# Gated linear attention in chunks of 64 tokens on 64x64 tensor-engine tiles, with slot outputs as the weights of the combining product

## The chip, the cores and the metric

The kernel runs on one core of a Trainium2 chip. The metric is the device time of one execution in microseconds. The kernel before was timed in three runs: median 246.3 us, from 245.9 to 248.71. All tensors are float32.

## The reference

Two stages. The first is a gated linear attention over 4 batches x 8 heads x 768 tokens, head width 48; the second a soft mixture of experts on its output (3072 tokens of 384 values, 32 slots, 8 experts of 4 slots, hidden width 1024).

```python
f = 1 / (1 + exp(-f_logit))
for t in range(768):
    state = f[:, :, t, :, None] * state + outer(k[:, :, t], v[:, :, t])    # 48 x 48 per head
    y[:, :, t] = q[:, :, t] @ state
x = y as (3072, 384)
logits = x @ phi                                    # (3072, 32)
d = softmax of logits over the tokens;  slot_input = d.T @ x
slot_out[e] = relu(slot_input[e] @ w1[e]) @ w2[e]   # 8 experts, 4 slots each
c = softmax of logits over the slots;   out = c @ slot_out
```

## The kernel before

**Chunks.** The recurrence is computed in blocks of 128 tokens of one batch, all 8 heads together: 4 batches x 6 blocks = 24 blocks, n = 0 to 23. With g the running sum of -log f inside a chunk (its rows are called gate sums here), the products of a chunk use k * exp(g) and q * exp(-g), so that the decay between two tokens comes out of one product. Heads go in four pairs `a`; of a pair, head `r` = 0 lies on partitions 0 to 63 and `r` = 1 on 64 to 127, 48 of the 64 rows used.

**One block** (function `block`, L382), by the names under which the steps are planned:

- `exp`, `ln` (L373, L376): log(1 + exp(-f_logit)) on ACT (ScalarE), for two blocks at once after the first two.
- `cum` (L396) and `cumT` (L401): the gate sums twice on PE (TensorE), by a triangle of ones: once with tokens on the partitions (one product of 384 columns), once with the head's rows on the partitions (four products).
- `g`, `p` (L404, L407): their exponentials on ACT, 384 and 512 wide.
- `mk` (L413), `mq` (L416), `ends` (L410): k times one, q times the other, and the chunk's last gate, on POOL (GpSimd).
- `tk` (L421), `pk` (L424): k is turned, four transposes on PE, and copied out of PSUM.
- `kv` (L443): k-v products of the chunk, weights of 128 tokens x 64 columns. `sa`, `sm` (L446, L450): the new state on DVE (VectorE), an addition and a multiplication by the last gate.
- `sc` (L431): scores, 128 x 128 per head, 64 rows x 128 columns of weights. `mask` (L436): two DVE multiplications by the triangle, 4 heads x 128 columns each.
- `ia` (L459): intra, masked scores (weights of 128 x 128) times v (48 columns). `ie` (L468): inter, q (weights of 64 rows x 128 columns) times the state before the block (48 columns), added in the same bank. `py` (L471), put_y, copies y out.
- `tx`, `px` (L505, L508) turn the block's tokens for the mixture.

**Units.** After each fourth block a unit of 512 tokens goes through the mixture's first part (`unit`, L513): logits (`lg`, L524), exponentials, two turns (L536), the slot sums (`pi`, L543), the softmax over the slots and its turn into `cts` (L599). The softmax over the tokens needs one maximum for all units: units 1 to 4 are joined to a running maximum, sum and slot sum as they come (`j_min` to `j_new`, L549 to L565), six small DVE and two ACT instructions each; unit 5 is kept apart and both are added in the tail (`psi`, L667).

**Tail** (`tail`, L634): common maximum, `psi`, the experts' first products (`up`, L706), relu, turns (L721), the second products in three column parts (`down`, L740), the sum over a slot's rows (L752), then `combine` (L769): for each of three parts and six units four products with `cts` as weights (128 x 128) and 128 columns of slot outputs streamed. `put_f` (L775) copies to SBUF and `store` (L783) writes.

**Memory.** PSUM has eight banks: two pairs (names `pr`: scores and y), three single ones (`sg`, for everything else) and one for `kv`. Twelve buffers of 1 MB (`hm`) take w1 during the loop; the seven arenas of the loop (`aq` to `ak`) take the first seven pieces of w2 as the loop sets them free, and the `hm` buffers the rest.

**What sets the order.** The instructions are not issued in loop order. Each step is entered in `Plan` (L75) with the engines that may do it, a cost on each, what it reads and writes and a priority; `schedule` (L116) takes the step that can start first, the priority deciding between near ties, picks the engine where two may do it, and the bank. The result is a fixed list per engine; each engine runs its list in order and waits by semaphores. All loads are issued by SP in one such list.

## Time and profile before

| | |
|---|---|
| median of three runs | 246.3 us (245.9 to 248.71) |
| profiled execution | 245.48 us, span 243.8 us, mean granted clock 0.945 |
| instructions | 6448, of them 2708 matmul records on PE |
| DMA | 50.89 MB, mean 209 GB/s |
| loads per block | q 256 KB, k 192 KB, v 192 KB, f 384 KB for two blocks |

The page of the profile lists busy time by engine; PEld is PE's weight loads, which overlap its products. A row of the order in time gives start and length in us, engine, line, operation, tiles (what it writes <- what it reads), for PE its array tile as rows*columns, the shape streamed, how many were merged, and in brackets how long the engine stood idle before and for whom. A group row ends in its total busy time, the mean ns of one, and the idle time before. An f32 product appears as two matmul records, a transpose as one. Records of products that run side by side in the array overlap, so the time of a group is read from its start to the next one's start, or from the span of many less the length of one.

### The profile page before, as it was taken

What the parts mean: (1) busy time and instruction counts of PE and PEld (TensorE: products, weight loads), DVE (VectorE), ACT (ScalarE), POOL (GpSimd) and SP (SyncE); (2) the same over time, 40 slices, a digit from 0 to 9 for tenths busy, and PEclk for the clock granted to TensorE, in tenths of its full rate; (3) what the DMA queues carried; (4) which work ended last, traced back from release to release, by engine and by line L of the source; (5) the groups of instructions that cost most, each with busy time, mean ns of one, the idle gap of its engine ahead of it and who ended that gap; (6) DMA issues with size and microseconds to landing.
All of it is one profiled execution on the core that took longest, in us unless ns stands there. A gap on an engine that the chain in (4) does not pass through costs nothing.

```text
span 243.8 us, 6448 instructions
## 1 busy us (share of the span) xinstructions
PE 230.1 (94%) x2708; PEld 190.1 (78%) x2708; DVE 103.2 (42%) x244; ACT 89.7 (37%) x193; POOL 57.7 (24%) x88
## 2 busy tenths in 40 slices
PE   8999999999999999999999999999988799999870
PEld 8789889878888789879897898888977333498760
DVE  3354543346443564357425485345370322224230
ACT  3454353436532255343524545433322211103330
POOL 2134432306320263213323431521400000000000
PEclk9999999999998999999999999999997569999965
DMA  6999366268753873366836663720785939905562
GB/s 177 350 347 332 120 189 226 84 218 249 259 170 108 265 246 125 105 179 270 242 116 197 239 221 125 235 79 3 272 321 203 376 95 378 421 12 205 238 264 88
DMA packets 17862, 50.89 MB, mean 209 GB/s; under 512 B 2336, under 2 KB 8736, under 8 KB 14752
## 3 DMA queue, kind: packets, MB, share of 16 engines
q1 hardware_dynamic: 17824, 50.39, 60.2%
q8 instruction: 23, 0.38, 0.6%
q14 instruction: 15, 0.12, 0.1%
HBM read 45.66 MB, written 4.72 MB: 207 GB/s over the span
## 4 chain that ended last, share of the span: by engine, by line
PE 93%; ACT 2%; DVE 1%; issue 1%; DVEq 0%
PE pr L459 17%; PE pr L431 10%; PE sg L401 10%; PE pr L468 9%; PE sg L396 8%; PE sg L706 5%; PE sg L443 5%; PE sg L740 5%; PE sg L421 5%; PE sg L769 4%; PE sg L505 4%; PE sg L306 3%; PE sg L524 2%; PE sg L543 2%; PE sg L599 1%; PE sg L721 1%
## 5 line engine op out<-in xcount | busy, mean ns | idle before, releaser
L459 PEld LDWEIGHTS pr<-av,as 128*128 128x128 f32 x384 | 45.0, 192 | 2.1 <-issue 1.0
L459 PE MATMUL pr<-av,as 128*128 128x48 f32 x384 | 45.8, 272 | 0.0
L436 DVE TENSOR_TENSOR as<-pr,tri 128x512 f32<-128x512 f32 x48 | 31.5, 686 | 28.2 <-PE pr L431 28.2
L401 PEld LDWEIGHTS sg<-tri,al 128*128 128x128 f32 x192 | 24.5, 196 | 3.6 <-issue 0.6
L401 PE MATMUL sg<-tri,al 128*128 128x128 f32 x192 | 27.2, 286 | 0.0
L468 PE MATMUL pr<-st,aq 64*128 64x48 f32 x320 | 22.5, 281 | 0.0
L396 PE MATMUL sg<-al,tri 128*128 128x384 f32 x48 | 21.2, 523 | 0.2 <-ACT al L376 0.2
L468 PEld LDWEIGHTS pr<-st,aq 64*128 64x128 f32 x320 | 19.9, 191 | 1.2 <-issue 0.2
L413 POOL TENSOR_TENSOR ap<-ak,gb 128x384 f32<-128x384 f32 x12 | 12.2, 1014 | 35.1 <-ACT gb L404 35.1
L471 ACT COPY xr<-pr 128x384 f32<-128x384 f32 x14 | 6.7, 479 | 32.7 <-PE pr L468 30.0
L471 DVE COPY xr<-pr 128x384 f32<-128x384 f32 x10 | 5.6, 558 | 25.4 <-PE pr L468 22.0
L413 POOL TENSOR_TENSOR ap<-ak 128x384 f32<-128x384 f32 x11 | 11.0, 1004 | 21.6 <-ACT ak L404 21.5
L421 PE MATMUL sg<-ident,ap 128*128 128x128 f32 x96 | 15.1, 280 | 0.3 <-DVE ap L413 0.3
L416 POOL TENSOR_TENSOR aq<-aq,af 128x512 f32<-128x512 f32 x11 | 14.0, 1272 | 0.0
L416 POOL TENSOR_TENSOR aq<-aq,ap 128x512 f32<-128x512 f32 x11 | 14.0, 1270 | 0.0
L443 PE MATMUL sg<-av,ap 128*64 128x48 f32 x320 | 13.9, 231 | 0.0
L431 PE MATMUL pr<-aq,ap 64*128 64x128 f32 x192 | 13.8, 284 | 0.0
L443 PEld LDWEIGHTS sg<-av,ap 128*64 128x64 f32 x320 | 11.3, 141 | 3.2 <-issue 2.3
L431 PE MATMUL pr<-aq,av 64*128 64x128 f32 x192 | 13.7, 282 | 0.0
L505 PE MATMUL sg<-ident,xr 128*128 128x128 f32 x72 | 12.8, 288 | 0.8 <-ACT xr L471 0.8
L431 PEld LDWEIGHTS pr<-aq,av 64*128 64x128 f32 x192 | 11.7, 188 | 2.1 <-issue 1.6
L508 ACT COPY xT<-sg 128x384 f32<-128x384 f32 x17 | 8.2, 480 | 12.9 <-PE sg L505 12.9
(144 smaller groups left out, 312.9 us busy)
## 6 DMA issues: line engine op xcount, KB each, us to landing
hm<-in_w_dram SPq DMA_DIRECT2D x17, 1024.0 KB, 7.9
aq<-in_q_dram SPq DMA_DIRECT2D x24, 256.0 KB, 3.1
ak<-in_k_dram SPq DMA_DIRECT2D x24, 192.0 KB, 4.1
av<-in_v_dram SPq DMA_DIRECT2D x24, 192.0 KB, 3.8
af<-in_f_dram SPq DMA_DIRECT2D x11, 384.0 KB, 4.5
out_dram<-hm SPq DMA_DIRECT2D x6, 512.0 KB, 3.0
out_dram<-hm SPq DMA_DIRECT2D x6, 256.0 KB, 3.1
af<-in_w_dram SPq DMA_DIRECT2D x1, 1024.0 KB, 4.8
```

Source lines behind the costliest of these rows:

```text
L396: nc.tensor.matmul(bank(("cum", n))[:, :384].rearrange("p (h d) -> p h d", h=H), tri, l[:, :, :D], start=True, stop=True)
L401: nc.tensor.matmul(pc[:, a], l[:, 2 * a : 2 * a + 2].rearrange("p r d -> p (r d)"), tri, start=True, stop=True)
L413: tt(e)(kp_[:, :, :D], k_, g_, op=ALU.mult)
L416: tt(e)(flat(q_), flat(q_), flat(p_), op=ALU.mult)
L421: nc.tensor.transpose(pk[:, a], kp_[:, 2 * a : 2 * a + 2].rearrange("p r d -> p (r d)"), ident)
L431: nc.tensor.matmul(ps[:, r, a], kt_[rs, a], q_[rs, a], start=True, stop=True)
L436: tt(e)(sc_[:, r], ps[:, r], tri.unsqueeze(1).broadcast_to([128, PR, 128]), op=ALU.mult)
L443: nc.tensor.matmul(pk[DP * r : DP * r + DP, a], kp_[:, 2 * a + r], v_[:, 2 * a + r], start=True, stop=True)
L459: nc.tensor.matmul(py[:, r, a], sc_[:, r, a], v_[:, 2 * a + r], start=a == 0, stop=first and a == PR - 1, skip_group_check=True,)
L468: nc.tensor.matmul(py[:, r, a], q_[rs, a], s_old[rs, a], start=False, stop=a == PR - 1, skip_group_check=True)
L471: copy(e)(x_.rearrange("p (a r e) -> p r a e", a=PR, r=2), y_at())
L505: nc.tensor.transpose(px[:, c], x_[:, 128 * c : 128 * c + 128], ident)
```

## The change

- **Chunk of 64.** `C` becomes 64; a block stays 128 tokens (`BT`) and holds two chunks. k comes from memory like q, with the head's rows on the partitions (padded from 48 to 64, so 256 KB per block).
- **64x64 tiles.** Gate sums, scores, k-v, inter and intra become 16 products per block each, on weights of 64 (or 48) rows x 64 (k-v: 48) columns. Chunk `c` and head `r` choose the quarter of the array: rows from one, columns from the other. [...]
- **Gate sums once.** `sums_l` replaces `cum` and `cumT`: only the form with the head's rows on the partitions, 64 columns per chunk; both exponentials read it, 512 wide each. `mk` multiplies k in place (512 wide); `tk` turns it for `kv`; the scores read k unturned.
- **State twice per block.** Two additions and two multiplications on DVE, one pair per chunk; `ends` takes two copies. One mask of 512 columns for two.
- **PSUM.** Three pairs (gate sums, k-v, y, scores share them) and two single banks; the pairs are zeroed at the start on DVE. `ie` now begins y's bank and `ia` ends it; scores are entered after `ie`.
- **No joins.** Each unit keeps its maximum, sum and slot sums; `psi` adds six units in the tail.
- **Combining.** `s4`, the slot outputs, becomes the weights (128 columns) and `cts` of four blocks is streamed, 512 columns: 18 products for 72. The output is stored transposed (384 x 3072).
- **Planner.** Costs of many steps change; six arenas instead of seven take pieces of w2.

```diff
-    plan = Plan({"pair": [0, 1], "one": [0, 1, 2], "kv": [3]})
+    plan = Plan({"pair": [0, 1, 2], "one": [0, 1]})
...
+    def c_kv(e):
+        for t in pairs:
+            nc.vector.memset(t, 0.0)
...
-        def cum(e):
-            nc.tensor.matmul(bank(("cum", n))[:, :384].rearrange("p (h d) -> p h d", h=H), tri, l[:, :, :D], start=True, stop=True)
-
-        def cumT(e):
-            pc = bank(("cumT", n)).rearrange("p (a t) -> p a t", a=PR)
-            for a in range(PR):
-                nc.tensor.matmul(pc[:, a], l[:, 2 * a : 2 * a + 2].rearrange("p r d -> p (r d)"), tri, start=True, stop=True)
+        def sums_l(e):
+            ps = bank(("cum", n))[:, :, : PR * C].rearrange("p c (a t) -> p c a t", a=PR)
+            for a in range(PR):
+                for c in range(2):
+                    for r in range(2):
+                        nc.tensor.matmul(ps[half[r], c, a], l_[half[c], 2 * a + r], tri[half[c]], start=True, stop=True)
...
         def scores(e):
...
-                    nc.tensor.matmul(ps[:, r, a], kt_[rs, a], q_[rs, a], start=True, stop=True)
+                        nc.tensor.matmul(ps[half[c], r, a], k_[rows[r], a, half[c]], q_[rows[r], a, half[c]], start=True, stop=True)
...
         def kv(e):
...
-                    nc.tensor.matmul(pk[DP * r : DP * r + DP, a], kp_[:, 2 * a + r], v_[:, 2 * a + r], start=True, stop=True)
+                for j in steps:
+                    for r in range(2):
+                        h, c = 2 * a + r, j ^ r
+                        nc.tensor.matmul(pk[C * r : C * r + D, j, a], kp_[half[c], h, :D], v_[half[c], h], start=True, stop=True)
...
         def inter(e):
...
-                    nc.tensor.matmul(py[:, r, a], q_[rs, a], s_old[rs, a], start=False, stop=a == PR - 1, skip_group_check=True)
+                for j in begun:
+                    for r in range(2):
+                        nc.tensor.matmul(py[half[j], r, a], q_[rows[r], a, half[j ^ r]], s_[j][rows[r], a], start=a == 0, stop=False, skip_group_check=True)
...
         def intra(e):
...
-                        py[:, r, a], sc_[:, r, a], v_[:, 2 * a + r], start=a == 0, stop=first and a == PR - 1, skip_group_check=True,
+                            py[half[j], r, a], sc_[half[c], r, a], v_[half[c], 2 * a + r], start=j not in begun and a == 0,
+                            stop=a == PR - 1, skip_group_check=True,
...
+        add(f"ie{n}", {"PE": 0.52}, inter, r=[*[S[j] for j in begun], Q, "kv0"], psum=("y", n), kind="pair", prio=T(n, 3.9))
+        add(f"sc{n}", {"PE": 0.52}, scores, r=[K, Q], psum=("sc", n), kind="pair", prio=T(n, 4), after=[len(plan.ops) - 1])
...
         def combine(p, x):
...
-                    nc.tensor.matmul(pf[:, g], cts[:, UB * x + g], s4[:, CUT[p] : CUT[p + 1]], start=True, stop=True)
+            return lambda e: nc.tensor.matmul(
+                bank(("cb", p, x))[:w], s4[:, CUT[p] : CUT[p + 1]], cts[:, UB * x : UB * x + UB].rearrange("p n t -> p (n t)"), start=True, stop=True,
+            )
```

How the order moves, at three places. A row gives line, operation, tiles with bank numbers, the shape written and how many stand together. First PE in the middle of the loop, before: turning k, k-v, gate sums, intra, inter, turning x and scores of neighbouring blocks alternate.

```order
L421 MATMUL sg_66<-ident,ap 128x128 x4
L443 MATMUL sg_67<-av,ap 64x48 x8
L396 MATMUL sg_64<-al,tri 128x384
L459 MATMUL pr_62<-av,as 128x48 x8
L468 MATMUL pr_62<-st_89,aq 128x48 x8
L401 MATMUL sg_65<-tri,al 128x128 x4
L396 MATMUL sg_66<-al,tri 128x384
L505 MATMUL sg_64<-ident,xr 128x128 x3
L431 MATMUL pr_63<-aq,av 128x128 x8
```

PE in the loop with the change (L403 gate sums, L429 turning k, L442 scores, L453 k-v, L472 inter, L482 intra, L521 turning x, L539 logits):

```order
L472 MATMUL pr_64<-st_90,aq 64x48 x2
L482 MATMUL pr_63<-av,ap 64x48 x16
L442 MATMUL pr_62<-aq,ak 64x64 x16
L521 MATMUL sg_65<-ident,xr 128x128 x3
L403 MATMUL pr_63<-tri,al 64x64 x16
L482 MATMUL pr_64<-av,ap 64x48 x16
L403 MATMUL pr_62<-tri,al 64x64 x16
L521 MATMUL sg_66<-ident,xr 128x128 x3
L403 MATMUL pr_64<-tri,al 64x64 x16
L429 MATMUL sg_65<-ident,ak 128x128 x4
L539 MATMUL sg_66<-xT,phs 32x128 x12
L453 MATMUL pr_63<-av,ap 48x48 x16
```

The groups on the pairs are all of 16 products now, some of them stand next to each other, and the gate sums of up to three blocks stand ahead of one block's k-v.

Second, DVE in the same part, before: masks two by two, and one state step (L446, L450) per block.

```order
L436 TENSOR_TENSOR as<-pr_63,tri 128x512 x2
L446 TENSOR_TENSOR sa<-sg_67,st_88 128x192
L450 TENSOR_TENSOR st_89<-sa,pend 128x192
L436 TENSOR_TENSOR as<-pr_62,tri 128x512 x2
L424 COPY av<-sg_65 128x512
L508 COPY xT<-sg_64 128x3x128
L446 TENSOR_TENSOR sa<-sg_67,st_89 128x192
```

DVE with the change (L445 mask, L456 and L461 the state's addition and multiplication, L524 the copy of turned x):

```order
L445 TENSOR_TENSOR ap<-pr_62,tri 128x512
L456 TENSOR_TENSOR sa_91<-pr_63,st_89 128x192
L461 TENSOR_TENSOR st_90<-sa_91,pend 128x192
L456 TENSOR_TENSOR sa_92<-pr_63,st_90 128x192
L461 TENSOR_TENSOR st_87<-sa_92,pend 128x192
L524 COPY xT<-sg_66 128x3x128
L445 TENSOR_TENSOR ap<-pr_64,tri 128x512
```

Between two blocks' masks stand four state instructions that read each other's results.

Third, PE in the tail, before: `down` (L740) of the next part and `combine` (L769) of the last, on three single banks.

```order
L740 MATMUL sg_66<-av,xr 32x128 x16
L769 MATMUL sg_64<-s_118,cts 128x128 x4
L769 MATMUL sg_65<-s_118,cts 128x128 x4
L740 MATMUL sg_66<-hm_75,xr 32x128 x16
L769 MATMUL sg_64<-s_118,cts 128x128 x4
```

PE in the tail with the change (L728 `down`, L753 `combine`):

```order
L728 MATMUL sg_65<-av,xr 32x128 x16
L753 MATMUL sg_66<-cts,s_118 128x512
L728 MATMUL sg_65<-hm_73,xr 32x128 x16
L753 MATMUL sg_66<-cts,s_118 128x512
L728 MATMUL sg_65<-hm_74,xr 32x128 x16
```

`down` holds one of the two single banks, and the combining products share the other.

## The prediction

> **What bounds the kernel now.** I read the page's busy shares and its chain of waits first, then the busy times by stage, then the order in time of TensorE in one stretch of the loop over blocks. The page:

> ```profile
> span 243.8 us, 6448 instructions
> ...
> PE 230.1 (94%) x2708; PEld 190.1 (78%) x2708; DVE 103.2 (42%) x244; ACT 89.7 (37%) x193; POOL 57.7 (24%) x88
> ...
> PE 93%; ACT 2%; DVE 1%; issue 1%; DVEq 0%
> ```

> TensorE (PE) is 93% of the chain that ended last; no other compute engine is busy for half the span. By stage (stretch and its length in us; busy time of PE, weight loads, DVE, ACT, POOL; then granted clock, DMA share, GB/s):

> ```profile
> 7.00:188.00 181.00, 178.52 (x2008) 154.30 (x2007) 85.72 (x197) 75.95 (x164) 55.47 (x69) 0.99 0.61 202
> 188.00:244.00 56.00, 45.67 (x668) 29.91 (x668) 15.44 (x41) 11.37 (x25) 0.40 (x1) 0.80 0.61 233
> 10.00:20.00 10.00, 9.79 (x107) 8.16 (x104) 5.62 (x11) 4.61 (x10) 2.99 (x4) 1.00 1.00 352
> ```

> The loop fills PE (178.5 of 181 us, clock 0.99) and leaves the others half idle. It begins with the first gate sum and ends with the last put_y:

> ```profile
> 7.16 0.81 PE L396 MATMUL sg<-al,tri 128*128 128x384 f32 x2
> ```

> ```profile
> 187.42 0.48 ACT L471 COPY xr<-pr 128x384 f32<-128x384 f32 x1 [2.83 <-PE pr L468]
> ```

> So the run is 7.2 us of start, 180.7 us of loop (7.16 to 187.90) and 55.9 us of mixture tail; the result lists 245.5 us for this execution, 1.7 more than its span and 0.8 under the median of 246.3. What a block costs PE is read from start to next start:

> ```profile
> 100.13 1.13 PE L431 MATMUL pr<-aq,av 64*128 64x128 f32 x16
> 101.19 0.66 PE L421 MATMUL sg<-ident,ap 128*128 128x128 f32 x4
> 101.68 0.49 PE L505 MATMUL sg<-ident,xr 128*128 128x128 f32 x3
> 102.10 0.67 PE L443 MATMUL sg<-av,ap 128*64 128x48 f32 x16
> 102.70 0.91 PE L396 MATMUL sg<-al,tri 128*128 128x384 f32 x2
> 103.45 1.88 PE L459 MATMUL pr<-av,as 128*128 128x48 f32 x16
> 105.26 0.86 PE L524 MATMUL sg<-xT,phs 128*32 128x128 f32 x24
> ```

> ```profile
> 122.67 1.09 PE L468 MATMUL pr<-st,aq 64*128 64x48 f32 x16
> 123.69 1.16 PE L401 MATMUL sg<-tri,al 128*128 128x128 f32 x8
> 124.69 0.60 PE L421 MATMUL sg<-ident,ap 128*128 128x128 f32 x4
> ```

> Scores 1.06, turning k 0.49, turning x 0.42, k-v products 0.60, gate sums 0.75 + 1.00, intra 1.81, inter 1.02. (An f32 product is two records, a turn one.) With k-v and inter in 20 of 24 blocks that is 6.9 us, 165 in all; the 15.6 left of the loop are the six units, 0.65 per block. The loop is the sum of PE's groups, with next to nothing waited for.

> **The change, part by part.** Intra is dear because its 128-column weights set the pace, not the 48 columns that it streams. What a 64-column tile costs is seen where two stand side by side in the array:

> ```profile
> L443 PE MATMUL sg<-av,ap 128*64 128x48 f32 x320 | 13.9, 231 | 0.0
> ...
> L667 PE MATMUL sg<-wd,pin 128*32 128x32 f32 x48 | 1.1, 245 | 0.3 <-ACT pin L546 0.3
> L740 PE MATMUL sg<-al,xr 128*32 128x128 f32 x32 | 1.1, 276 | 0.0
> ```

> 16 records of L443 span 0.67 and one lasts 0.231: (0.67 - 0.231)/15 = 29 ns per record, 58 for the two that run together. The change cuts rows too, so four 64x64 tiles can stand together: 58/4 = 14.6 ns per record. Each of the five groups (gate sums, scores, k-v, inter, intra) has 16 products, 32 records: 0.47 us, and with the 0.13 that L443 loses at its ends (0.60 - 0.47) 0.60. The trace has no 64x64 tile; that four run as two do is an assumption, which the rivals take up. Five groups 3.0, turns 0.49 + 0.42, units 0.65: 4.6 us, less 0.1 for the halves missing at each sequence's ends; 4.46 x 24 = 107 us. Lower, if neighbours of one tile shape lose less between them. These two groups start 0.90 apart, of which 32 records at (1.08 - 0.276)/31 = 26 ns are 0.83:

> ```profile
> 213.01 1.08 PE L740 MATMUL sg<-ak,xr 128*32 128x128 f32 x32
> 213.91 1.06 PE L740 MATMUL sg<-af,xr 128*32 128x128 f32 x32
> ```

> At 0.05 lost in place of 0.13, and k-v's 48-column weights at three quarters of 64, PE falls to 95. In the new order about half of the neighbours share a shape: I take 101 (95 to 107).

> The other engines inherit the loop. ACT, DVE and POOL rows that bear on it:

> ```profile
> L407 ACT ACTIVATE af<-sg 128x512 f32<-128x512 f32 x12 | 7.2, 597 | 11.1 <-PE sg L401 9.4 <-POOL ap L413 1.7
> ...
> L404 ACT ACTIVATE gb<-sg 128x384 f32<-128x384 f32 x12 | 5.9, 491 | 10.6 <-PE sg L396 9.9 <-POOL pend L410 0.6
> ```

> ```profile
> L436 DVE TENSOR_TENSOR as<-pr,tri 128x512 f32<-128x512 f32 x48 | 31.5, 686 | 28.2 <-PE pr L431 28.2
> L450 DVE TENSOR_TENSOR st<-sa,pend 128x192 f32<-128x192 f32 x16 | 7.1, 442 | 1.6
> L446 DVE TENSOR_TENSOR sa<-sg,st 128x192 f32<-128x192 f32 x16 | 5.7, 354 | 5.4 <-PE sg L443 5.3
> ```

> ```profile
> L416 POOL TENSOR_TENSOR aq<-aq,ap 128x512 f32<-128x512 f32 x11 | 14.0, 1270 | 0.0
> L413 POOL TENSOR_TENSOR ap<-ak,gb 128x384 f32<-128x384 f32 x12 | 12.2, 1014 | 35.1 <-ACT gb L404 35.1
> ...
> L410 POOL COPY pend<-af 128x4 f32<-128x4 f32 x12 | 2.8, 233 | 37.6 <-ACT af L407 37.6
> ```

> ACT: the gate exponentials go from 384 to 512 wide (24 x 0.106 = 2.5) and the order gives it five more put_y at 0.48, while the joins' eight small exponentials go: 76 becomes about 79. DVE: 24 masks fewer (-16.5), 24 state additions (+8.5) and 22 state multiplications (+9.7) more, the joins' 24 instructions gone (at L446's 0.354, -8): 86 becomes some 80. POOL: k is 512 wide (24 x 0.26 = 6) and the ends take two copies (5.6): 55 becomes 67. DMA: 24 blocks of q and k (256 KB each), v and f (192 KB each) and 12 MB of w1 are 34 MB, at the 352 GB/s of 10:20 some 97 us. So behind PE's 101 stand DMA with 97, DVE and ACT with 80: a loop that had one limit has two, with two more at 80%.

> PE will therefore not be busy throughout. Block 0 now takes from 7.2 to this row's end:

> ```profile
> 15.89 0.48 ACT L471 COPY xr<-pr 128x384 f32<-128x384 f32 x1 [0.83 <-PE pr L459]
> ```

> These are 9.2 us of handing on, in which the new PE has little more than one block's 4.2 us to do: 4 us idle in front, some 3 at the end. In between I put 4 to 5 us of waits: the order on each engine is fixed, POOL's 1.27 stands once ahead of the block's k and once ahead of its q, and every second block brings ACT a double exponential ahead of a gate sum. 101 + 11.5 = 112.5. What is late next is the side that PE waited on last: inter reads the state after two additions and two multiplications in a row on DVE (0.8 us per pair), with masks, and so intra, queued behind them.

> The start stays at 7.2: PE's warm products end there, and DVE's added memsets (three pairs of 1024 columns, at L436's rate about 4 us) end before. Without that cover they would cost what they overrun.

> In the tail psi adds all six units where two stood, 96 records more:

> ```profile
> 194.86 0.55 PE L667 MATMUL sg<-wd,pin 128*32 128x32 f32 x24
> ```

> ```profile
> 190.00:200.00 10.00, 8.44 (x97) 3.77 (x93) 4.16 (x19) 1.88 (x7) 0.40 (x1) 0.51 0.60 216
> ```

> (0.55 - 0.245)/23 = 13 ns each, at half the clock: +1.3 us. Combining has 18 products that stream 512 columns where 72 streamed 128. With 128-column weights one of the 72 costs about L459's 1.81/16 = 0.11, 8 us in all; one of the 18 costs no less than that (2 us) and no more than L396's 0.375 per record for 384 columns would give at 512, 0.5 (9 us). Their copies out of PSUM stay 18, on two single banks instead of three, so I take -0.5 (-4 to +1). w2's pieces and the stores keep their places behind the same steps.

> Sum: 7.2 + 112.5 + 55.9 + 1.3 - 0.5 + 1.7 = **178.1 us**.

> **Rivals.** *The fixed order binds* (0.22). Three PSUM pairs hold four things of each block: the gate sums (PE 0.6, two exponentials of 0.6), k-v (0.6, then 0.35, 0.44, 0.35 on DVE), y (inter 0.6, scores 0.6, mask 0.69, intra 0.6, put_y 0.48) and the scores (0.6, mask 0.69). With 0.15 for each handover, an assumption, that is 2.1 + 2.1 + 3.6 + 1.5 = 9.3 us, or 3.1 per block on three pairs, three quarters of PE's 4.2; loads at 97 of 101 leave even less. If these queue up and DMA gets three quarters of 352 GB/s, the loop is 130 us and the time 196. For it: every share rises. Against: none exceeds PE's.

> *PE alone binds* (0.15): 96 us and 7 at the ends, 168. So far PE's work hid every wait; but then the others had half their time.

> *The tiles run, but fewer at once* (0.07). L740's 26 ns per record may be a floor for a record and not its 128 columns: 160 records x 11.3 ns x 24 = +43, 221. Two at a time, 29 ns: +56, 234. Against: L667 starts records 13 ns apart, and that at half the clock. [...]

> *The tiles run one after the other* (0.03), and the change doesn't do what it says: if row tiles and column tiles can't be mixed, a record costs 58 ns, +44 x 160 x 24 = +169: 347, slower. This decides from 14.6 + 68,000/(160 x 24) = 32 ns per record on; L443's 29 for two tiles speaks against it.

> The forecast keeps 0.53.

> **How the numbers follow.** The forecast's own range is 170 to 188 (PE 95 to 107, idle time 9 to 17, tail -4 to +1). With the PE-bound and the queueing case, 166 to 199 leaves out just under 2 in 10. Faster by over 2% (about what a measurement of this kernel tells from no change) is all but the serial case and accidents of its size: 0.95; within 2% 0.02, slower 0.03.

> **What would show it.** Right: groups of 32 records on 64x64 tiles 0.5 to 0.6 us apart; PE busy near 100 us in a loop of 105 to 120; DVE and ACT near 70% busy in it, DMA share above 0.8; a tail of 56 to 58 us. Wrong: records 25 ns or more apart; gaps before PE's groups that together pass 20 us, ended by DVE's state steps, ACT's gate exponentials or loads; a granted clock in the loop well under 0.99, as the tail's 0.51 already is.

## The result, and the profile after

The changed kernel takes 235.0 us (median of four runs, 231.4 to 236.3) where the kernel before takes 246.3: a ratio of 0.944 (95% interval 0.929 to 0.960). It is faster, but by a sixth of what was forecast: 178 us, with a range of 166 to 199. The profiled execution is the longest of the four, 236.26 us. The ratios leave out executions more than 1.5% above the fastest of their kernel; of these four that leaves 231.4 and 234.8.

First the page of the changed kernel: span, busy times, granted clock in 40 slices, the queue that brings instructions, and the chain that ended last.

```profile
span 234.5 us, 10707 instructions
...
PE 179.6 (77%) x4814; PEld 133.6 (57%) x4814; DVE 101.0 (43%) x231; ACT 95.6 (41%) x203; POOL 69.7 (30%) x113
...
PEclk9955595699855999958678579999997589999985
...
q8 instruction: 40, 0.66, 1.1%
...
PE 63%; issue 15%; DVE 13%; ACT 5%; DVEq 0%; POOLq 0%
```

The same two rows of the page before:

```profile
PEclk9999999999998999999999999999997569999965
...
q8 instruction: 23, 0.38, 0.6%
```

Three things are new. PE is busy for 77% of the span instead of 94%. Its clock, 0.99 in the loop before, drops to half again and again (a 5 in the row PEclk, 0.80 over the loop). And 15% of the chain is "issue", time in which PE waits for nothing that the profile shows. PE's products and weight loads have gone from 2 x 2708 to 2 x 4814, and the queue that brings code moves 40 packets of 16 KB for 23.

By stage (columns: stretch and its length, busy time of PE, weight loads, DVE, ACT, POOL, granted clock, DMA share, GB/s), with the loop's last put_y as the border:

```profile
7.00:173.00 166.00, 130.21 (x4069) 104.18 (x4068) 85.56 (x188) 78.53 (x169) 67.53 (x95) 0.80 0.65 217
173.00:234.50 61.50, 43.52 (x710) 23.66 (x710) 11.11 (x33) 14.65 (x30) 0.40 (x1) 0.85 0.63 247
```

The loop takes 166 us (forecast 112.5): PE is busy 130.2 (forecast 101) and idle 35.8 (forecast 11.5). ACT and POOL have the work that was forecast (79 and 67), DVE some 6 us more than its 80. What PE waited for, all lines with "issue" in the loop (L655 and L728 belong to the tail), and the two largest other waits (engine, what it was to write, line, what ended the wait: us in total, times, longest):

```profile
PE pr L403 <- issue: 8.7, 5, 3.2
PE pr L482 <- issue: 5.2, 3, 2.5
PE pr L472 <- issue: 5.0, 3, 1.9
PE sg L655 <- issue: 4.0, 1, 4.0
PE pr L482 <- DVE ap L445: 3.8, 10, 0.8
PE sg L521 <- issue: 3.6, 1, 3.6
PE pr L472 <- DVE st L461: 2.8, 3, 1.5
PE sg L728 <- issue: 1.9, 1, 1.9
...
PE pr L442 <- issue: 1.0, 1, 1.0
PE sg L539 <- issue: 0.9, 1, 0.9
...
PE pr L453 <- issue: 0.8, 1, 0.8
```

The loop's issue waits are 8.7 + 5.2 + 5.0 + 3.6 + 1.0 + 0.9 + 0.8 = 25.2 us, in 15 stops. That leaves 10.6 us of idle time of every other kind, nearly the 11.5 of the forecast. The clock explains the rest. Six stretches of the loop are at half clock, and their lengths (17.07, 10.24, 13.66, 6.83, 6.83 and 10.24 us) are whole multiples of 3.41 us. The first two, and the sum of the six:

```profile
11.34:28.41 17.07, 13.89 (x321) 12.13 (x322) 8.10 (x16) 7.08 (x14) 7.70 (x9) 0.50 0.78 284
35.23:45.47 10.24, 7.77 (x179) 6.29 (x175) 4.26 (x8) 3.56 (x8) 7.83 (x11) 0.50 0.69 246
...
sum 64.87, PE 53.27 PEld 42.12 DVE 25.07 ACT 23.12 POOL 31.61; mean PE 8.88 PEld 7.02 DVE 4.18 ACT 3.85 POOL 5.27
```

PE is busy there for 53.3 us. If the same work takes half of that at full clock (an estimate; stage G below shows 213 ns per record at 0.50 for 112 before the fall), 26.6 us are lost, and 130.2 - 26.6 = 103.6 is an estimate of what the loop's work costs at full speed: the forecast's 101. So the 53.5 us by which the loop missed are 25 us of stops, 27 us of half clock, and 1 to 2 us of everything else.

What a stop looks like, in the order in time of PE:

```profile
65.97 1.10 PE L403 MATMUL pr<-tri,al 64*64 64x64 f32 x32
66.85 0.86 PE L453 MATMUL pr<-av,ap 64*48 64x48 f32 x32
67.64 0.47 PE L521 MATMUL sg<-ident,xr 128*128 128x128 f32 x1
71.73 0.69 PE L521 MATMUL sg<-ident,xr 128*128 128x128 f32 x2 [3.62 <-issue]
```

The three turns of L521 are one step: same input, same output tile, same semaphores. After the first, PE stops for 3.62 us and goes on. Nothing in the program stands between the two. Counted from the start, the stops lie at PE's instruction (products, weight loads and the semaphore instructions between them) 450, 706, 1218, 1474, 2497, 2754, 3010, 3777 and so on: distances of 256 or a multiple, give or take one. A packet of queue q8 has 16 KB (40 move 0.66 MB), and PE mostly resumes 1.2 to 1.5 us after one has landed; that one packet holds the 256 instructions, 64 bytes each, is an estimate from these distances and sizes. (The expectations below speak of 34 us of stops within groups: there the whole distance from record to record was counted, here only the idle time.)

### The profile page after: what moved, and what is told of

Read it like the earlier page. It is cut to its first block, busy times and chain, and to the rows that moved or that the text cites. A ratio compares the mean times of both kernels' runs of the same rounds, so it can differ in the third digit from the quotient of the medians.

```text
span 234.5 us, 10707 instructions
## 1 busy us (share of the span) xinstructions
PE 179.6 (77%) x4814; PEld 133.6 (57%) x4814; DVE 101.0 (43%) x231; ACT 95.6 (41%) x203; POOL 69.7 (30%) x113
## 4 chain that ended last, share of the span: by engine, by line
PE 63%; issue 15%; DVE 13%; ACT 5%; DVEq 0%; POOLq 0%
PE pr L403 8%; PE pr L482 7%; PE sg L429 6%; PE pr L442 6%; PE pr L472 5%; PE sg L694 5%; PE sg L728 5%; PE sg L521 5%; DVE ap L445 3%; PE pr L453 3%; PE sg L539 3%; PE sg L316 3%; PE sg L753 2%; DVE st L461 2%; ACT hm L759 2%
## 5 line engine op out<-in xcount | busy, mean ns | idle before, releaser
L421 POOL TENSOR_TENSOR ak<-ak,av 128x512 f32<-128x512 f32 x11 | 14.0, 1269 | 55.0 <-ACT av L407 28.0
L403 PE MATMUL pr<-tri,al 64*64 64x64 f32 x768 | 22.4, 259 | 8.9 <-issue 8.7
L424 POOL TENSOR_TENSOR aq<-aq,pt 128x512 f32<-128x512 f32 x22 | 28.7, 1303 | 0.4 <-ACT pt L407 0.4
L482 PE MATMUL pr<-av,ap 64*64 64x48 f32 x768 | 20.2, 247 | 9.1 <-issue 5.2
L472 PE MATMUL pr<-st,aq 48*64 48x48 f32 x704 | 20.3, 240 | 8.0 <-issue 5.0
L403 PEld LDWEIGHTS pr<-tri,al 64*64 64x64 f32 x768 | 18.4, 166 | 12.3 <-issue 11.5
L482 PEld LDWEIGHTS pr<-av,ap 64*64 64x64 f32 x768 | 16.8, 158 | 14.2 <-DVE ap L445 7.7
L445 DVE TENSOR_TENSOR ap<-pr,tri 128x512 f32<-128x512 f32 x24 | 16.6, 690 | 19.1 <-PE pr L442 18.7
L472 PEld LDWEIGHTS pr<-st,aq 48*64 48x64 f32 x704 | 17.1, 153 | 12.4 <-issue 7.3
L442 PE MATMUL pr<-aq,ak 48*64 48x64 f32 x768 | 20.2, 241 | 1.0 <-issue 1.0
L461 DVE TENSOR_TENSOR st<-sa,pend 128x192 f32<-128x192 f32 x38 | 19.7, 519 | 2.5
L429 PE MATMUL sg<-ident,ak 128*128 128x128 f32 x96 | 19.6, 344 | 1.4 <-DVE ak L421 1.4
L456 DVE TENSOR_TENSOR sa<-pr,st 128x192 f32<-128x192 f32 x40 | 14.2, 355 | 14.6 <-PE pr L453 7.1
L521 PE MATMUL sg<-ident,xr 128*128 128x128 f32 x72 | 15.5, 328 | 5.1 <-issue 3.6
L442 PEld LDWEIGHTS pr<-aq,ak 48*64 48x64 f32 x768 | 17.1, 152 | 3.3 <-issue 3.3
L421 POOL TENSOR_TENSOR ak<-ak,af 128x512 f32<-128x512 f32 x12 | 15.3, 1271 | 11.7 <-issue 8.4
L453 PE MATMUL pr<-av,ap 64*48 64x48 f32 x704 | 15.5, 224 | 0.8 <-issue 0.8
L429 PEld LDWEIGHTS sg<-ident,ak 128*128 128x128 f32 x96 | 13.1, 172 | 3.2 <-DVE ak L421 1.6
L521 PEld LDWEIGHTS sg<-ident,xr 128*128 128x128 f32 x72 | 8.9, 161 | 9.6 <-issue 3.9
L407 ACT ACTIVATE pt<-pr 128x512 f32<-128x512 f32 x24 | 14.3, 597 | 0.0
```

Of the source, the lines that this page charges most:

```text
L403: nc.tensor.matmul(ps[half[r], c, a], l_[half[c], 2 * a + r], tri[half[c]], start=True, stop=True)
L407: nc.scalar.activation(dst.rearrange("p a (c t) -> p c a t", c=2), src, AF.Exp, scale=sign)
L421: tt(e)(flat(k_), flat(k_), flat(g_), op=ALU.mult)
L424: tt(e)(flat(q_), flat(q_), flat(p_), op=ALU.mult)
L429: nc.tensor.transpose(pk[:, a], k_[:, a], ident)
L442: nc.tensor.matmul(ps[half[c], r, a], k_[rows[r], a, half[c]], q_[rows[r], a, half[c]], start=True, stop=True)
```

## Experiments

In these, a piece is 256 PE instructions. The theory to be tested: PE's code arrives piece by piece, and the dense tiles use it up faster than it comes; the stops in turn bring the clock down. The rivals: the tiles themselves lower the clock; transfers alone delay the code; or PE's work and ordinary waits set the time.

### Products alone, without the kernel

> This kernel computes nothing of the reference: it only runs stages of products on PE and stores zeros. Stages, with 24 or 32 full-array products of 256 columns between them: A, 512 products on 64x64 tiles, 64 columns each; B, 256 on 64x64 tiles, 128 columns; C, 192 on 64x64 tiles, 256 columns; D, 160 full-array products of 64 columns; E, eight rounds of 24 and then eight of 8 full-array products, PE waiting for three DVE copies (about 1.6 us) after each round; F, as A, while 12 MB are loaded and 4.7 MB stored. Supply theory (PE's instructions arrive in pieces of 256, one per 3.4 us at best): A stops after every 256 PE instructions (weight loads and products counted) without any wait or transfer in sight, and its 2048 instructions take 8 x 3.4 = 27 us where 29 ns per product would give 15; B is near the limit and C does not stop; C runs at a granted clock of 1.0; in E the short rounds run at half clock although they use no tiles; F is like A or up to 2 us per piece slower. Rival, the tiles themselves lower the clock: C at 0.5 too, E at 1.0. Rival, only transfers delay the instructions: A takes 15 us without a stop, F alone stops. Rival, stops come from the waits of the real kernel: neither A nor F stops.

The core of it, the form of the gate sums:

```python
c, r = i // 2 % 2, i % 2
nc.tensor.matmul(ps[x + c][64 * r : 64 * r + 64, :n], wt[64 * c : 64 * c + 64, 64 * r : 64 * r + 64],
                 mv[64 * c : 64 * c + 64, :n], start=True, stop=True)
```

Stages A and F in the order in time:

```profile
25.93 2.09 PE L88 MATMUL ps<-mv,wt 64*64 64x64 f32 x128 [1.91 <-issue]
29.93 2.09 PE L88 MATMUL ps<-mv,wt 64*64 64x64 f32 x128 [1.91 <-issue]
33.93 2.09 PE L88 MATMUL ps<-mv,wt 64*64 64x64 f32 x128 [1.91 <-issue]
...
262.84 3.32 PE L88 MATMUL ps<-mv,wt 64*64 64x64 f32 x128 [2.79 <-issue]
269.58 3.36 PE L88 MATMUL ps<-mv,wt 64*64 64x64 f32 x128 [3.42 <-issue]
275.78 3.64 PE L88 MATMUL ps<-mv,wt 64*64 64x64 f32 x128 [2.84 <-issue]
```

128 product records come with 128 weight loads: one piece. With no load and no wait anywhere (4 GB/s in the row of A below), PE works 2.09 us and stops for 1.91: 4.0 us per piece, 64 instructions per us (the last two pieces of the stage come 3.7 us apart). With loads (stage F) a piece takes 6.2 to 6.7 us. The same stages by stretch (PE, weight loads, DVE, POOL, then clock, DMA share, GB/s): A, B (128 columns), F.

```profile
24.00:44.00 20.00, 10.47 (x643) 9.79 (x640) 0.00 (x0) 0.00 (x0) 1.00 0.02 4
60.00:71.00 11.00, 11.00 (x414) 11.00 (x407) 0.00 (x0) 0.00 (x0) 1.00 0.02 4
262.00:302.00 40.00, 22.02 (x813) 21.06 (x816) 0.00 (x0) 0.00 (x0) 0.63 0.99 403
```

B streams twice the columns per instruction and does not stop: its four pieces take 14.2 us, 3.5 each. So code came at up to 73 instructions per us where PE did not run into its end, and at 64 to 69 in A, where it did. C and D (256 columns; full array with 64) have 0.0 us of idle time, and C, on tiles, keeps its clock at 1.00, against the rival that the tiles lower it. So the supply limit is real without any transfer, against the other two rivals. A piece also takes longer under load, which the transfer rival had right in part. The clock: with 1.9 us of every 4.0 idle A stays at 1.00; with 2.55 to 3.42 us idle in pieces of 6.2 to 6.7 F falls to 0.63. It isn't the traffic as such: the kernel before ran at 1.00 under 352 GB/s (its stretch from 10 to 20 us). Stage E was a miss: with 1.1 us of idle time in every 3.2 its clock stayed at 1.0.

### Fewer instructions for more work, and the tail's product

> The changed kernel with the gate sums as 4 products of 128x128 weights against a block-diagonal 128x128 triangle in place of 16 on 64x64 tiles: per block 16 PE instructions (loads and products) for 64, 1152 fewer in the loop, and about 0.5 us more of PE's own time (1.00 for 0.50), 12 us in all. Supply theory: 4.5 pieces of 256 at 3.4 us, 15 us less supply time, and fewer stops, so also more time at full clock: 215 to 230 us in spite of PE's 12 us more work, stops within groups down from 34 us to under 25. Rival, PE's own work and ordinary waits set the loop: 245 to 250, slower than the changed kernel's 235. Rival, tiles lower the clock: some gain from clock, but stops within groups stay near 34 us.

```diff
-                for c in range(2):
-                    for r in range(2):
-                        nc.tensor.matmul(ps[half[r], c, a], l_[half[c], 2 * a + r], tri[half[c]], start=True, stop=True)
+                nc.tensor.matmul(ps[:, a], l_[:, 2 * a : 2 * a + 2].rearrange("p r d -> p (r d)"), tri2, start=True, stop=True)
...
-        add(f"cum{n}", {"PE": 0.52}, ...
+        add(f"cum{n}", {"PE": 1.0}, ...
```

225.8 us (223.7 to 228.8), 0.916 of the kernel before (0.908 to 0.924): 9 us faster than the changed kernel by the medians, 7 by the ratios, though each block's gate sums take PE 0.99 us from start to start where 32 records on small tiles take 0.5 at full clock (stage A: 128 in 2.09). The rival's 245 to 250 is out. What PE waited for falls to 5.4 and 3.6 us of issue at the two largest lines, and the loop ends at 167.0.

> As the kernel with wide gate sums, and psi in the tail as 18 products on 128x128 weights (32 columns streamed) in place of 72 on 128x32 tiles: 216 PE instructions fewer in a stage that took 6.3 us, most of it a stop. Supply theory: psi 2 to 4 us, total 2 to 4 us under the kernel with wide gate sums alone. Rival (psi's cost is its products at half clock): no gain, since a full-array product costs about what four tiles side by side do.

```diff
-                    for g in range(4):
-                        nc.tensor.matmul(ps[32 * g : 32 * g + 32, c], pin[:, x, 128 * c + 32 * g : 128 * c + 32 * g + 32], wd[:, x], ...)
+                    nc.tensor.matmul(ps[:, c], pin[:, x, 128 * c : 128 * c + 128], wd[:, x], ...)
```

234.5 us (230.9 to 237.0): worse by 9, by the ratios (0.940 for 0.916) by 6. The row of psi here, and the one of the kernel with wide gate sums, both at half clock:

```profile
179.22 7.89 PE L653 MATMUL sg<-wd,pin 128*128 128x32 f32 x36 [1.12 <-DVE wd L645]
```

```profile
173.75 2.15 PE L654 MATMUL sg<-wd,pin 128*32 128x32 f32 x144 [1.04 <-DVE wd L645]
```

A quarter of the instructions cost 5.7 us more: full-array records start 213 ns apart at half clock with 32 columns streamed, and stage G below shows the same 213 ns with 48, so that the columns streamed don't set it; on 128x32 tiles, in the other row, a record takes (2.15 - 0.24)/143 = 13 ns at the same clock. The expectation that fewer instructions help here was wrong; psi did not stop in the kernel with wide gate sums, so its 4.0 us stop in the changed kernel hung on where the pieces fell. In these two profiles the loop, too, ends at 173.0 for 167.0 us, with the same instructions in the same order. But this profile is of one of two long executions (236.3 and 237.0); the two short ones, 230.9 and 232.7, exceed the wide kernel's 225.8 by about what psi costs. Why executions of one kernel scatter by 6 us is open.

### Is it the order?

> The changed kernel with the planner's cost of a gate sum step at 1.0 in place of 0.52: nothing but the order of steps changes, to the order that the kernel with wide gate sums has; its products stay 16 on 64x64 tiles. It tells what of the 9 us between the changed kernel (235.0) and the one with wide gate sums (225.8) came from the order. Supply theory: 232 to 239, no gain. Rival, the order gave the gain: 224 to 228.

```diff
-        add(f"cum{n}", {"PE": 0.52}, ...
+        add(f"cum{n}", {"PE": 1.0}, ...
```

237.5 us (236.8 to 237.7), 0.965 of before. The order of the wide kernel with the small tiles gains nothing; with the wide products in the same order it is 11.6 us faster. So the gain belongs to the products.

### More work in the same instructions

> The changed kernel with 128 columns streamed by each gate sum product in place of 64 (the triangle stands twice side by side, the second half of each result isn't read): the same number of PE instructions, and by the probe's stages A and B about 27 ns per product record group where there were 14.6, so 0.45 us more PE work per block, 11 us in all. Supply theory: PE waits for its code in these groups anyway, so the added work takes the place of stops and keeps the clock up: 225 to 238 us against 235, stops within groups 5 us or more below 34. Rival, PE's work at its clock sets the loop: 246 to 250.

```diff
-                        nc.tensor.matmul(ps[half[r], c, a], l_[half[c], 2 * a + r], tri[half[c]], start=True, stop=True)
+                        nc.tensor.matmul(ps[half[r], c, a], l_[half[c], 2 * a + r], tri2[half[c]], start=True, stop=True)
```

227.8 us (226.3 to 229.6), 0.927 of before (0.920 to 0.934). This kernel does everything that the changed kernel does and streams 64 columns more in each of 384 products, for nothing, and all its four runs are faster than all four of the changed kernel, by 7 us in the medians and 4 by the ratios. The gate sums' group (busy, mean ns of one, idle time before them), changed kernel and this one:

```profile
L403 PE MATMUL pr<-tri,al 64*64 64x64 f32 x768 | 22.4, 259 | 8.9 <-issue 8.7 <-ACT al L378 0.2
```

```profile
L405 PE MATMUL pr<-tri,al 64*64 64x128 f32 x768 | 30.2, 291 | 4.4 <-issue 4.2 <-ACT al L380 0.2
```

8 us more busy, 4.5 less stopped: by itself this group costs more. The gain lies in the clock of the whole loop. The stretch from 7 to 160 us of the changed kernel, then of double_sums, of the wide sums, of the order alone:

```profile
7.00:160.00 153.00, 120.70 (x3714) 96.39 (x3714) 76.24 (x162) 74.52 (x161) 65.69 (x92) 0.79 0.67 227
```

```profile
7.00:160.00 153.00, 125.20 (x4008) 101.43 (x4004) 85.01 (x187) 76.94 (x166) 67.62 (x95) 0.92 0.69 234
```

```profile
7.00:160.00 153.00, 123.84 (x3296) 104.34 (x3298) 90.17 (x188) 71.64 (x151) 68.98 (x96) 0.89 0.69 234
```

```profile
7.00:160.00 153.00, 127.67 (x3717) 102.36 (x3706) 86.76 (x180) 70.60 (x149) 67.31 (x93) 0.77 0.66 227
```

The clock separates the two kernels at 226 to 228 us (0.92, 0.89) from the two at 235 to 238 (0.79, 0.77). PE's busy time hardly differs (120.7 to 127.7 us): 32 gate sum records take 0.88 us at half clock (65.97 to 66.85 in the rows above) and about 0.5 at full, so that work at half clock counts nearly double in it. But the clock alone doesn't rank kernels, as the next run shows.

> The changed kernel with 128 columns streamed in gate sums and scores in place of 64 (half of each result isn't read): the same PE instructions, by the probe 0.45 us more PE work per group, 22 us in all. With the gate sums alone doubled it took 227.8. Supply and clock theory: the second doubling fills more of the stops and keeps more windows at full clock, 221 to 229. Rival, after the first doubling PE's work sets the loop: 236 to 240.

```diff
-                        nc.tensor.matmul(ps[half[c], r, a], k_[rows[r], a, half[c]], q_[rows[r], a, half[c]], start=True, stop=True)
+                        q2 = q_[rows[r], a].rearrange("p (c t) -> p c t", c=2)
+                        nc.tensor.matmul(ps[half[c], r, a].rearrange("p (c t) -> p c t", c=2), k_[rows[r], a, half[c]], q2[:, ::-1] if c else q2, start=True, stop=True)
```

236.9 us (234.7 to 239.6), 0.959 of before: the rival. The clock is a little better still (0.93 up to 160 us), but the losses don't shrink any more. That shows when each profiled loop, from the first gate sum to the last put_y, is split as the changed kernel's was above (us; work and loss by the same estimate):

| kernel | loop | work at full clock | lost at half clock | stops | other idle time |
|---|---|---|---|---|---|
| changed | 166.0 | 103.6 | 26.6 | 25.2 | 10.6 |
| order alone | 166.3 | 102.0 | 36.5 | 12.1 | 15.7 |
| wide sums | 158.8 | 112.5 | 15.5 | 10.9 | 19.9 |
| double_sums | 155.9 | 115.6 | 11.6 | 16.5 | 12.1 |
| double_both | 167.2 | 126.3 | 11.5 | 17.6 | 11.9 |

From double_sums to double_both 10.7 us of work are added, nothing is saved, and the loop grows by 11.3. The row of the order alone says more: it has half the changed kernel's stops and 10 us more of half clock, so the two losses change places; its four executions, at mean clocks from 0.78 to 0.84, lie within 1 us. The 0.88 us of a group at half clock are 73 instructions per us, the pace of the code in stage B; by this estimate a PE at half clock would hardly run into the end of its code. And against that same order the wide products save 21 us of half clock, and stops hardly at all.

> The kernel with wide gate sums (225.8 us), and 128 columns streamed in the scores in place of 64: the same PE instructions, 11 us more PE work. Supply and clock theory: still stops of 13 us and a mean clock of 0.89 to be had, 220 to 227. Rival, PE's work sets the loop by now: 234 to 238.

The same doubling of the scores on the wide gate sums: 228.5 us (223.2 to 236.6) for 225.8, too scattered to tell a gain from a loss. The expected 234 to 238 of a PE-bound loop is not reached either.

### What the transfers do

> The changed kernel with an eighth of each w1 buffer loaded (256 of 2048 columns, and the experts' first products read these 256 repeatedly: the rest of w1 is left out of the computation), so 10.5 MB of 52.7 MB fewer, nearly all of it in the loop. Supply theory: the stops stay at every 256 PE instructions, but the longest (3.2 to 4.0 us) shrink to the usual 1 to 2: 5 to 12 us less, 223 to 230 us, clock still below 0.9 in the loop. Rival, transfers delay the instructions and that is all: stops within groups under 8 us, loop near 120 us, 185 to 195 us. Rival, neither: 235.

```diff
-        return lambda e: nc.sync.dma_start(t, w1[x])
+        return lambda e: nc.sync.dma_start(t[:, :256], w1[x][:, :256])
```

221.5 us, one run of a kernel that leaves out seven eighths of w1: 13.4 less than the changed kernel, more than the supply theory gave and far from the 185 to 195 of transfers alone. The loop ends at 156.7. Its issue waits are 6.6 us at the gate sums and 2.6 and 1.6 at intra and the turns, 13.7 in 14 stops for 25.2 in 15; up to 160 us it moves 172 GB/s for 227, at a clock of 0.89 for 0.79. So with fewer transfers the stops were shorter, but without most of w1 they are still there.

> The kernel with wide gate sums (225.8 us), each 1 MB load of w1 issued as four loads with rows of 2 KB in place of one with rows of 8 KB. If long rows ahead of it delay the code: stops within groups from 13 us to 8 or less in the first 90 us, 215 to 222 us. If the amount of traffic does: 224 to 228. If SP's additional issues hold back q, k and v: above 228.

```diff
-        return lambda e: nc.sync.dma_start(t, w1[x])
+        return lambda e: [nc.sync.dma_start(t[:, 512 * y : 512 * y + 512], w1[x][:, 512 * y : 512 * y + 512]) for y in range(4)]
```

225.5 us (219.5 to 227.3) for 225.8: no difference shown.

> The kernel with wide gate sums (225.8 us), the loads of w1 spread over the loop, one per two blocks, where they now crowd its first half (294 to 307 GB/s up to 80 us, 128 after 120 us). Supply theory with contention: pieces of code come faster in the first half and no slower than now in the second, loop 5 to 12 us shorter, 213 to 222 us. Rival, loads don't matter as long as they are in time: 224 to 228. Rival, w1's last pieces now arrive after the loop: the experts' products wait, above 228.

```diff
-        ... w=[("home", x)], prio=1e3 + x, bytes=128 * HOME * 4)
+        ... w=[("home", x)], prio=1e3 + x, bytes=128 * HOME * 4, after=[next(o["n"] for o in plan.ops if o["name"] == f"mask{2 * x}")])
```

229.1 us (225.6 to 229.4): a miss, no gain from spreading the loads. The amount of traffic mattered here (less_loads: 221.5 us), its place in the loop doesn't show.

### What brings the clock down

> This kernel computes nothing of the reference. Stages on PE: G, 128 full-array products of 48 columns without a stop (the form that intra had before the change); H, 192 transposes of 128x128; then three times 448 products on 64x64 tiles with 64 columns (7 pieces of 256 instructions), each while the same 12 MB are loaded: in 12 loads with rows of 8 KB, 48 with rows of 2 KB, 96 with rows of 1 KB. In the first probe a piece took 4.0 us without loads and 6.2 with rows of 8 KB. If the code's transfer waits behind the descriptors ahead of it: the piece's time falls with the rows, to about 4.6 us at 2 KB and 4.3 at 1 KB. If it waits for its share of a busy memory: 6.2 in all three, as long as the loads run. Clock: if half clock follows from windows in which PE was idle, G and H stay at 1.0; if the form of the products counts, G or H falls to 0.5 without any stop.

Stages G and H by stretch, and the three with loads (rows of 8, 2 and 1 KB):

```profile
23.00:64.00 41.00, 41.00 (x196) 41.00 (x196) 0.00 (x0) 0.00 (x0) 0.50 0.00 0
81.00:98.00 17.00, 17.00 (x158) 17.00 (x157) 0.00 (x0) 0.00 (x0) 1.00 0.00 1
...
110.00:145.00 35.00, 20.56 (x822) 19.30 (x825) 0.00 (x0) 0.00 (x0) 0.68 0.88 362
168.00:200.00 32.00, 18.13 (x814) 17.17 (x814) 0.00 (x0) 0.00 (x0) 0.73 0.95 329
224.00:250.00 26.00, 15.63 (x826) 14.80 (x819) 0.00 (x0) 0.00 (x0) 0.87 0.73 209
```

G is the surprise: PE is busy in every moment and runs at half clock. A column takes 0.84 ns at full clock (the 256 columns of the products in between: 216 ns from start to start), so 48 columns stream for 40 of the 112 ns that such a product takes at full clock, before the fall (213 after it). With 64 columns (stage D of the first probe: 54 of 112 ns) the clock stayed at 1.0. So idle time alone doesn't tell where the clock falls, G having none; that the share of a 3.41 us step in which columns stream does is an estimate, from G's 40 of 112 ns and D's 54. The pieces with loads took about 6.2, 5.8 and 4.4 us, but with the rows the traffic fell too (362, 329, 209 GB/s), so rows and amount are not told apart here; wide_small speaks for the amount, as far as its scatter allows.

> This kernel computes nothing of the reference and loads nothing while PE works. Five stages of 320 products (1280 PE instructions, five pieces) on four tiles, the forms that the changed kernel has: tiles of 64x64 with 64 columns (gate sums), 64x64 with 48 (intra), 48x64 with 64 (scores), 48x64 with 48 (inter), 64x48 with 48 (k-v); 32 full-array products of 256 columns between them. Supply theory: all five stop at every 256 instructions and take 4.0 us per piece, since the code's arrival and not the products set the pace. Clock: if only the length of a stop counts, all five stay at 1.0 as the first did in the first probe; if the share of the time in which columns are streamed counts (full-array products of 48 columns fell to 0.5 without a stop, those of 64 did not), the three stages of 48 columns fall to 0.5.

All five forms stop at every 256 instructions, at about 3.5 to 4.0 us per piece (issue waits of 5.6, 3.7, 6.6, 2.0 and 7.2 us in the order of the stages). Two of them by stretch, gate sums (64x64 tiles, 64 columns) and inter (48x64, 48 columns, a stretch before and one after the clock falls):

```profile
20.55:34.20 13.65, 8.08 (x506) 7.54 (x500) 0.00 (x0) 0.00 (x0) 1.00 0.02 5
...
109.30:116.10 6.80, 5.58 (x234) 4.92 (x233) 0.00 (x0) 0.00 (x0) 1.00 0.01 2
116.13:129.80 13.67, 12.92 (x420) 12.33 (x420) 0.00 (x0) 0.00 (x0) 0.50 0.02 5
```

Gate sums stay at 1.0 with PE busy for 59% of the time (8.08 of 13.65 us). Inter's form falls after the first step with a stop in it, PE busy for 82% of the stretch before (5.58 of 6.80). Intra's and k-v's forms fall a step or two later, the scores' in the last step. So in these stages neither the length of the stops nor the form of the products decides alone: A and F, one form, differ by their stops (1.9 us at 1.00, 2.55 to 3.42 at 0.63), gate sums and inter by rows and columns. An estimate: columns streamed at 0.84 ns, times the share of the array's rows and columns that a tile uses, fill 0.43 to 0.50 of the time in the gate sums' form and 0.48 in stage D, which kept the clock, and 0.36 in G and 0.24 to 0.37 in the four forms that lost it. A share of very roughly 0.4 parts these stages; in the changed kernel's loop the steps before a fall have PE busy for 29 to 66%, but some of 62 to 65% were not followed by one, so the exact measure is open.

## Why the prediction was wrong, point by point

| term, us | forecast | measured |
|---|---|---|
| start | 7.2 | 6.9 |
| PE busy in the loop | 101 | 130.2 (103.6 at full clock, + 26.6) |
| PE idle in the loop | 11.5 | 35.8 (25.2 issue, 10.6 other) |
| tail | 55.9 + 1.3 - 0.5 = 56.7 | 61.5 |
| outside the span | 1.7 | 1.8 |

**The tiles: right.** Two groups of 32 records each in a stretch at full clock, with what follows them:

```profile
56.90 0.57 PE L453 MATMUL pr<-av,ap 64*48 64x48 f32 x32
57.30 0.36 PE L482 MATMUL pr<-av,ap 64*64 64x48 f32 x9
58.28 0.50 PE L482 MATMUL pr<-av,ap 64*64 64x48 f32 x20 [0.62 <-issue]
```

k-v's group takes 0.40 here from start to start, for the 0.47 of the prediction's sum; in stage A, on 64 columns, 128 records take 2.09 us and one 0.25, so (2.09 - 0.25)/127 = 14.5 ns per record. Four tiles stand together at the 14.6 ns that were assumed. That ends the rivals of fewer tiles at once, of a floor at L740's 26 ns and of tiles one after the other. Intra, in the last two rows, is cut by a stop after 9 of its 32 records.

**The waits of the fixed order: right in sum, in part by luck.** 10.6 us of idle time beside the stops, for 11.5. But it is made up differently: in front 2.6 us for 4 (PE is busy 6.66 of the 9.27 us from 7.00 to 16.27), so more in between; and in the other kernels of the table the same kind of time comes to 12 to 20. The queueing rival (196 us) came nearer to the result, but for a reason that isn't there: masks and state steps end 3.8 + 2.8 = 6.6 us of PE's idle time, in waits of at most 1.5 us. Its 0.15 per handover was an assumption; two handovers of the kernel before, by the profile's ends, took 0.03 (L401 to L407, 13.70 to 13.73) and 0.12 (L431 to L436, 120.82 to 120.94).

**The step that failed** is "101 + 11.5 = 112.5". It took PE's rate as set by the array alone and put nothing for the supply of code. Group by group the 0.47 us for 32 records was right, but it is 64 instructions in 0.47 us, 136 per us, and code came at 64 to 73 per us without traffic: the loop's 8137 instructions are 32 pieces, 111 us at 3.5 each, 127 at 4.0, 197 at 6.2, and 140 at the 4.4 of probe2's stage with 209 GB/s, near the loop's own 217. By this estimate the supply alone, with the loop's loads, put 112.5 out of reach. The profile before could not show this limit, since its 2 x 2708 PE instructions in 243.8 us are far from it; but its queue q8 was there to be read, and the prediction counted records and not what feeds them. The other half of the miss is the clock: I kept 0.99 for the loop, though the tail's 0.51 stood in the prediction, and only listed "a granted clock in the loop well under 0.99" among the signs against it. That sign came (0.80), and so did the one on gaps of over 20 us, but what ended them was code and not "DVE's state steps, ACT's gate exponentials or loads".

**The tail** missed by 4.8 us, 3.7 of them in psi. Before, psi's two groups took from 194.86 to 196.16, 1.3 us:

```profile
195.68 0.55 PE L667 MATMUL sg<-wd,pin 128*32 128x32 f32 x24 [0.28 <-ACT pin L546]
196.16 0.59 PE L681 MATMUL sg<-zr,same 128*128 128x1 f32 x2
```

With the forecast's 1.3 more that is 2.6; it took 6.3 (179.3 to 185.6). The price per record held, (2.14 - 0.24)/142 = 13 ns, but a piece ends before psi's last record:

```profile
179.34 2.14 PE L655 MATMUL sg<-wd,pin 128*32 128x32 f32 x143 [1.19 <-DVE wd L646]
185.48 0.21 PE L655 MATMUL sg<-wd,pin 128*32 128x32 f32 x1 [3.99 <-issue]
```

**What is shown, and what isn't.** That code supply stops PE is shown (stage A: 1.91 us of stop in every 4.0 without loads; the stops in the middle of groups, at every 256 instructions or a multiple, mostly ended 1.2 to 1.5 us after a packet of code). That PE's own work did not set the loop's time is shown by wide_sums and double_sums, where more work cost less time. That longer stops went with a lower clock is shown in the probe (A against F, the same instructions: stops of 1.9 us at 1.00, of 2.55 to 3.42 at 0.63). That the loop's 26.6 us of half clock come from the stops alone is not: the 48-column forms fell to 0.50 in probe3 where the gate sums' form stayed at 1.00, the order alone gave more half clock with half the stops, and the two were not taken apart in the whole kernel. How much of the clock's share belongs to which stays open, as does the scatter of executions: the split above is of the changed kernel's longest one, at a mean clock of 0.82, and the other three had 0.83 to 0.86.

## What to carry to other kernels

Count PE's instructions, not only their work: weight loads and products together, against what it got here, 64 to 73 per us without other traffic (stages A and B) and about 40 at 403 GB/s (stage F, 256 in 6.2 to 6.7 us). Where small tiles pass that rate, put more into each instruction (a block-diagonal weight, more columns per product) even at the cost of array time, as long as that saves more stops and half clock than it adds: wide_sums, at 225.8 us, does the gate sums with a quarter of the instructions in twice the array time, while doubling the scores on top of the gate sums cost 9 us again. And don't take a full clock for granted: stops of 2.55 us and more in pieces of 6.2 (stage F, 0.63) and full-array products of 48 columns without a stop (stage G, 0.50) both went with a lower one.
